# Attention with two mixtures of experts on one core: exponentials issued last in their step on ScalarE, and the placing product of v's block sums moved one step later into a bank of its own

## The chip, the cores and the metric

The kernel runs on one core of a Trainium2 chip. The metric is device microseconds (us) of one execution; lower is better.

## The reference

Three layers follow one another: a windowed attention, a soft mixture of experts over its output (3072 tokens of width 512, 32 slots), and a second mixture that sends each token to one expert. The change touches the attention and the first accumulation of the soft mixture, which runs along with it. What they compute:

```python
batch, n_heads, seq, head_dim = (4, 8, 768, 64)
block, window = (32, 16)
k_sum = k.reshape(B, H, nb, block, D).max(axis=3)      # nb = 24 blocks
v_sum = v.reshape(B, H, nb, block, D).mean(axis=3)
scores_l = scale * np.matmul(q, k.transpose(0, 1, 3, 2))   # masked to |i-j| < window
scores_s = scale * np.einsum('bhsd,bhnd->bhsn', q, k_sum) + np.log(block)
scores_all = np.concatenate([scores_l_m, scores_s], axis=-1)
a = np.exp(scores_all - np.max(scores_all, axis=-1, keepdims=True))
a = a / (np.sum(a, axis=-1, keepdims=True) + 1e-09)
attn = np.matmul(a, np.concatenate([v, v_sum], axis=2))
...
logits = x @ phi                        # soft mixture, x = attn as tokens
d = np.exp(logits - logits.max(0, keepdims=True))      # over all tokens
slot_input = (d / (d.sum(0, keepdims=True) + 1e-9)).T @ x
```

## The kernel before, in words

The 32 pairs of batch and head are taken two heads at a time: 16 pairs `n`, each cut into two halves of 384 rows. A half is a step `u` (0 to 31, pair `n = u // 2`), so even steps begin a pair. Ten more steps drain the pipeline and finish the soft mixture's slot inputs; after them come the expert weights' products and the second mixture, which the diff doesn't touch.

The order of instructions on each engine is the order in which the program issues them (a manual schedule). Each engine works through its own queue in that order, and an instruction that waits for data holds up all that stand behind it on the same engine. In the code, the loop over `u` calls in turn:

- `s_pe(u)`, line 302: 12 scores products on PE (24 matmul instructions, since one in this type takes two) into two banks, one for each head; they read q, and the windows of k together with the block maxima that `t_sum` has put into k's tile.
- `s_max(u, j)`, line 317: on DVE, scaling, mask and row minimum of the negated scores, three for each head, into the SBUF buffer `sms[u % 2]`.
- `s_exp(u, j)`: the row minimum is subtracted on POOL (line 330), then ScalarE takes the exponential (line 333), for each head.
- `v_pe(u - 2)`, line 354, and `v_norm(u - 2)`, lines 369 to 371: the product po of the transposed weights with v, and DVE's division by the sums.
- In odd steps, `vs(n)` and `vs2(n)` for the next pair but the current: `vs_pe` (line 249) sums v's blocks in 24 instructions into a bank `pv`; `vs_out` (line 257) copies that out on ScalarE; `vs_dist` (line 260) is a product with a 0/1 matrix that places each sum in the rows where it is needed, and writes to columns 256 to 385 of the same bank; a second `vs_out` copies that out, and `vs_in` (line 268) copies it into v's tile on POOL.
- `x_pe`, `x_ev`, `x_log`, lines 387, 397 and 405: transposes of the finished rows, ScalarE's copy, and the logits of the soft mixture.
- Once in eight steps the soft mixture's pieces: `moe_a` (steps 13, 21, 29, 37: column maxima, exponential, copy of the logits, correction of the running sum), `moe_b` (transposes of that, one step later), `moe_c` (product with the tokens, two steps after that), `moe_d`.
- `p_pe(u - 1)`, lines 341 and 342: transposes of the previous step's exponentials, and ScalarE's copies of them (`pts`).
- `t_sum(n + 1)` in odd steps, lines 277 to 286: on DVE the block maxima of the next pair's keys, in two levels; line 285 writes the part that the next step's first scores read, line 286 the rest.

PSUM banks: three in rotation (`ps_tr`, tag `tr`) for pv, the transposes and moe_b's and moe_c's products; three for the scores; one for po; one for the logits. A new tile waits until the one three before it has been read.

Loads are issued by SyncE (SP) in the same loop: keys, queries and v three pairs ahead, and one 1 MB tile of expert weights in most even steps from step 4 on; a load waits for its buffer's last reader.

Of the kernel before, what the change touches and what calls it, by code (L numbers as in the profile page):

```python
# [11 lines left out]
F32 = mybir.dt.float32  # L12
# [10 lines left out]
P = 128  # L23
B, H, S, D = 4, 8, 768, 64
# [28 lines left out]
C_DIST = C_BLK + 72  # L53
# [81 lines left out]
def tile_kernel(ctx, tc, qT, kTd, vwd, phi, w1, w2, emb, tau, u1, u2, consts, consts2, out):  # L135
    nc = tc.nc

    cp = ctx.enter_context(tc.tile_pool(name="cp", bufs=1))
    con = cp.tile([P, C_END], F32, name="con")
# [5 lines left out]
    nm_run = cp.tile([96, B], F32, name="nm_run")  # L145
# [58 lines left out]
    with ExitStack() as es:  # L204
        p3 = es.enter_context(tc.tile_pool(name="p3", bufs=3))
        p2 = es.enter_context(tc.tile_pool(name="p2", bufs=2))
        ps_tr = es.enter_context(tc.tile_pool(name="ps_tr", bufs=3, space=PSUM))
# [4 lines left out]
        st_ = {}  # L212
        NPAIR = B * 4
# [5 lines left out]
        sms = [fix[3][:, i * 6 * KW : (i + 1) * 6 * KW].rearrange("p (j c x) -> p j c x", j=2, c=3) for i in range(2)]  # L219
# [34 lines left out]

        def vs_out(n, i):
            sm = st_["vo", n]
            nc.scalar.copy(sm[:, 130 * i : 130 * i + 130], st_["pv", n][:, 256 * i : 256 * i + 130])  # L257

        def vs_dist(n):
            nc.tensor.matmul(  # L260
                st_["pv", n][:, 256:386], con[:, C_DIST : C_DIST + P], st_["vo", n][:, 0:130], start=True, stop=True
            )

        def vs_in(n):
            vo = st_.pop(("vo", n))
            for row0, par in ((32, 0), (96, 1)):
                eng = nc.vector if n == 0 and par else nc.gpsimd
                eng.tensor_copy(  # L268
                    st_["vw", n][row0 : row0 + NB, par].rearrange("p (s x) -> p s x", s=6),
                    vo[row0 : row0 + NB, 130:260].unsqueeze(1).to_broadcast([NB, 6, 130]),  # L270
                )
# [53 lines left out]
                    accum_out=st_["nb", u][:, j, c : c + 1],  # L325
                )

        def s_exp(u, j):
            sm = sms[u % 2][:, j]
            nc.gpsimd.tensor_tensor(  # L330
                out=sm, in0=sm, in1=st_["nb", u][:, j].unsqueeze(2).to_broadcast([P, 3, KW]), op=ALU.subtract
            )
            nc.scalar.activation(sm, sm, AF.Exp, scale=-1.0)  # L333

        def p_pe(u):
            pts = p2.tile([KW, 2, 3, P], F32, tag="pts", name=f"pts{u}")
            for j in range(2):
                pt = ps_tr.tile([P, 512], F32, tag="tr", name=f"pt{u}_{j}")[:KW, 0 : 3 * P]
                pt = pt.rearrange("p (c x) -> p c x", c=3)
                for c in range(3):  # L340
                    nc.tensor.transpose(pt[:, c, :], sms[u % 2][:, j, c, :], ident)  # L341
                nc.scalar.copy(pts[:, j], pt)  # L342
            st_["pts", u] = pts
# [69 lines left out]
        def moe_a(b):  # L413

            lp = st_.pop(("lp", b))
            LT = p2.tile([96, 2, 256], F32, tag="LT", name=f"LT{b}", bufs=1)
            nm, prev = nm_run[:, b : b + 1], nm_run[:, b - 1 : b]
            nc.vector.tensor_reduce(nm, lp, axis=AX.X, op=ALU.max, negate=True)
            if b:
                nc.vector.tensor_tensor(out=nm, in0=nm, in1=prev, op=ALU.min)  # L420
            nc.scalar.activation(LT[:, 1, :], lp, AF.Exp, bias=nm, scale=1.0, accum_out=sm_run[:, b : b + 1])
            nc.vector.tensor_copy(LT[:, 0, :], lp)
            if b:
                al = sp.tile([96, 1], F32, tag="al", name=f"al{b}")
                nc.scalar.activation(al, prev, AF.Exp, bias=nm, scale=-1.0)
                nc.vector.scalar_tensor_tensor(
                    out=sm_run[:, b : b + 1],
                    in0=sm_run[:, b - 1 : b],
                    scalar=al,
                    in1=sm_run[:, b : b + 1],  # L430
                    op0=ALU.mult,
                    op1=ALU.add,
                )
                st_["al", b] = al
                if b == B - 1:
                    dal = p3.tile([96, 96], F32, name="dal", bufs=1)
                    nc.vector.tensor_scalar_mul(dal, ident[:96, :96], al)
                    st_["dal"] = dal
            st_["LT", b] = LT

        def moe_b(b):
            LT = st_.pop(("LT", b))
# [8 lines left out]
        def moe_b_ev(b):  # L451
            L = sp.tile([P, 2, 2, 96], F32, tag="L", name=f"L{b}")
            pn = st_.pop(("pn", b))
            if b < B - 1:
                nc.vector.tensor_copy(L, pn)
            else:
                nc.vector.tensor_copy(L[:, 1], pn[:, 1])
                nc.scalar.copy(L[:, 0], pn[:, 0])
            st_["L", b] = L
# [120 lines left out]
        def keep_warm(n):  # L580

            pw = ps_o.tile([P, 3, 2, 65], F32, tag="po", name="warm1").rearrange("p a b x -> p (a b x)")
            for _ in range(n):
                nc.tensor.matmul(pw[:, 0:256], ident, con[:, C_MASK : C_MASK + 256], start=True, stop=True)  # L584

        def at(u, first, every, count):

            i, r = divmod(u - first, every)
            return i if r == 0 and 0 <= i < count else None
# [7 lines left out]
        last = B - 1  # L597

        def vs(n):
            vs_pe(n)  # L600
            vs_out(n, 0)

        def vs2(n):
            vs_dist(n)
            vs_out(n, 1)
            vs_in(n)

        for u in range(NU + 11):
            inr = lambda w: 0 <= w < NU
            m, odd = divmod(u, 2)  # L610
            if inr(u):
                s_pe(u)
                for j in range(2):
                    s_max(u, j)
                    s_exp(u, j)
            if inr(u - 2):
                if (u - 2) % 8 == 0:
                    st_["X", (u - 2) // 8] = xp.tile([P, 6, DM], F32, tag="X", name=f"X{(u - 2) // 8}")
                v_pe(u - 2)
                v_norm(u - 2)  # L620
            if u == 1:
                p_pe(0)
                vs(0)
                vs2(0)
                vs(1)
                vs2(1)
            vn = m + 1 if odd and 0 < m < NPAIR - 1 else None
            if vn is not None:
                vs(vn)
            if (n := at(u, 3, 2, NPAIR)) is not None:  # L630
                x_pe(n, 0)
                x_ev(n, 0)
            if (n := at(u, 4, 2, NPAIR)) is not None:
                x_pe(n, 1)
                x_ev(n, 1)
            if (n := at(u, 6, 2, NPAIR)) is not None:
                x_log(n)
            if (b := at(u, 13, 8, B)) is not None:
                moe_a(b)
            if (b := at(u, 14, 8, B - 1)) is not None:  # L640
                moe_b(b)
                moe_b_ev(b)
            if (b := at(u, 16, 8, B - 1)) is not None:
                moe_c(b)
                moe_c_ev(b)
            for i in range(3):
                if (b := at(u, 16 + i, 8, B)) is not None:
                    moe_d(b, i)
            if vn is not None:
                vs2(vn)  # L650
            if inr(u - 1) and u > 1:
                p_pe(u - 1)
            if odd and m + 1 < NPAIR:
                t_sum(m + 1)
            if u == U_END:
                keep_warm(2)
                si_max()
                si_max_ev()
                keep_warm(1)
                moe_b(last)  # L660
                moe_c(last, 0)
                keep_warm(1)
                moe_b_ev(last)
                si_bc()
                si_bc_ev()
                moe_c(last, 1)
                si_den()
                si_den_ev()
                moe_c(last, 2)
                moe_c_ev(last)  # L670
                keep_warm(1)
                siT_done()
                keep_warm(1)
            if u == 0:
                load_qk(2)
                load_v(2)
            if odd and m < NPAIR - 3:
                load_qk(m + 3)
                load_v(m + 3)
            if u == 3:  # L680
                nc.sync.dma_start(out=con[:, C_SEL:], in_=consts[:, C_SEL:])
                nc.sync.dma_start(out=phis, in_=phi.rearrange("(c p) s -> p c s", p=P))
            for _ in range(W_STEPS.count(u)):
                load_w()
# [128 lines left out]
    for r in range(2):  # L813
        for fc in range(8):
# [4 lines left out]
            for c in range(2 if late else 1):  # L819
                cs = slice(c * 256, c * 256 + 256) if late else slice(0, DM)  # L820
                for g in range(4):
# [4 lines left out]
                        start=(r, fc) in ((0, 0), (1, G_STEP + 1)),  # L826
                        stop=(r, fc) in ((1, G_STEP), (1, 7)),
# [19 lines left out]
            if r == 0 and fc % 2:  # L847
                b = fc // 2
# [4 lines left out]
            if 8 * r + fc in C_STEPS:  # L853
                b, j = divmod(C_STEPS.index(8 * r + fc), 2)
# [526 lines left out]
```

## Time and profile before

| what | value |
|---|---|
| runs of the kernel, median (lowest to highest of 3) | 293.59 us (292.58 to 293.78) |
| profiled execution, its own time | 292.89 us |
| span of the profiled execution | 291.1 us |
| mean granted TensorE clock | 0.958 of full speed |
| busy share of the span: PE, DVE, ACT, POOL | 84%, 53%, 44%, 31% |
| scores of step 2 start, scores of step 31 start | 16.81 us, 156.23 us |
| first product of the expert weights starts | 179.86 us |

Engines are PE (TensorE matmul), PEld (its weight loads, which overlap), DVE (VectorE), ACT (ScalarE), POOL (GpSimd) and SP. An instruction's row gives its start, its duration, engine, line, operation, what it writes and reads, and in brackets the time that its engine stood idle before it with the instruction that ended the wait. Matmuls are pipelined, so the duration of a group of them reaches into the next group; the distance from start to start tells what a group costs. Steps are cut at the first scores product (line 302): step 15 is 76.29 to 81.42.

### The profile page before, as it was taken

The numbers are of one execution on the slowest core, as the hardware profiler recorded it, in microseconds if no ns is written. First come the engines' busy times: TensorE is split into PE (matmuls) and PEld (weight loads), VectorE is DVE, ScalarE is ACT, GpSimd is POOL, SyncE is SP. The second block draws the span as 40 slices with busy tenths as digits, with TensorE's granted clock in tenths as the row PEclk, the third lists the DMA queues.
The fourth block names the chain that finished last, engine by engine and source line by source line (L and its number), as shares of the span: only waits on it lengthen the run. The fifth ranks groups of instructions, "written<-read, shape, count | busy, mean of one in ns | idle before, by whom it ended". The sixth has DMA issues, their size and how long they took to land.

```text
span 291.1 us, 7899 instructions
## 1 busy us (share of the span) xinstructions
PE 245.6 (84%) x3070; PEld 158.4 (54%) x3070; DVE 153.7 (53%) x699; ACT 127.7 (44%) x289; POOL 91.5 (31%) x131
## 2 busy tenths in 40 slices
PE   5688889896798886889868889999989999769980
PEld 1467666665566764656656454333256673536760
DVE  2366676666657666766666243115121467565850
ACT  1425655564454663355544331103322647923540
POOL 0455546554445544537444010000010272010000
PEclk9979999999999999999989799999999979986997
DMA  7997989999488996863485799999939200001993
GB/s 221 404 350 256 369 274 324 334 352 313 163 301 265 312 306 257 281 226 111 146 257 196 274 359 371 351 386 386 331 108 375 102 0 1 1 27 44 338 381 113
DMA packets 33658, 72.53 MB, mean 249 GB/s; under 512 B 2712, under 2 KB 4504, under 8 KB 33616
## 3 DMA queue, kind: packets, MB, share of 16 engines
q1 hardware_dynamic: 33552, 71.77, 70.1%
q8 instruction: 26, 0.43, 0.6%
q0 software_dynamic: 64, 0.20, 0.2%
q14 instruction: 16, 0.13, 0.1%
HBM read 65.67 MB, written 6.29 MB: 247 GB/s over the span
## 4 chain that ended last, share of the span: by engine, by line
PE 37%; DVE 5%; ACT 4%; DMA 3%; issue 2%; POOL 2%; SPq 1%; DVEq 0%; ACTq 0%; POOLq 0%
PE ph L746 5%; PE pO L822 4%; PE pht L1039 3%; DMA w2e<-in_moe_w_dram 3%; PE py L1282 2%; PE py L1284 2%; PE py L1283 2%; PE po L354 2%; DVE hlo L1052 2%; POOL fix L330 2%; PE s L302 1%; PE pa L476 1%; PE warm L584 1%; PE pc L194 1%; PE tx L387 1%
## 5 line engine op out<-in xcount | busy, mean ns | idle before, releaser
L333 ACT ACTIVATE fix<-fix 128x360 f32<-128x360 f32 x64 | 32.3, 504 | 74.9 <-POOL fix L330 74.9
L330 POOL TENSOR_TENSOR fix<-fix,nb 128x360 f32<-128x360 f32 x64 | 49.2, 789 | 48.0 <-DVE nb L317 48.0
L317 DVE CUSTOM_DVE_ANT_0 fix<-s,con 128x120 f32<-128x120 f32 x192 | 41.7, 279 | 40.5 <-PE s L302 39.3
L354 PE MATMUL po<-vw,pts 120*64 120x65 f32 x768 | 33.9, 236 | 7.3 <-ACT pts L342 6.7
L354 PEld LDWEIGHTS po<-vw,pts 120*64 120x64 f32 x768 | 27.8, 145 | 15.1 <-ACT pts L342 10.3
L268 POOL COPY vw<-vw 24x780 f32<-24x780 f32 x31 | 26.3, 848 | 28.1 <-issue 26.7
L342 ACT COPY pts<-pt 120x384 f32<-120x384 f32 x64 | 27.8, 483 | 6.2 <-PE pt L341 5.0
L341 PE MATMUL pt<-con,fix 128*120 128x128 f32 x192 | 27.9, 279 | 2.2 <-ACT xT L397 1.5
L341 PEld LDWEIGHTS pt<-con,fix 128*120 128x120 f32 x192 | 21.2, 138 | 9.4 <-issue 5.8
L302 PE MATMUL s<-fix,fix 64*64 64x120 f32 x480 | 18.4, 277 | 4.6 <-DVE fix L285 4.2
L387 PE MATMUL tx<-con,X 128*128 128x128 f32 x96 | 18.0, 298 | 0.7 <-DVE X L371 0.7
L371 DVE TENSOR_TENSOR X<-po,den 128x384 f32<-128x384 f32 x32 | 17.8, 558 | 1.1
L302 PEld LDWEIGHTS s<-fix,fix 64*64 64x64 f32 x480 | 13.4, 136 | 8.5 <-DVE fix L285 4.8
L1052 DVE CUSTOM_DVE_ANT_0 hlo<-pht,scr 128x1024 fp32r<-128x1024 f32 x11 | 13.3, 1212 | 8.6 <-PE pht L1039 8.5
L397 ACT COPY xT<-tx 128x384 f32<-128x384 f32 x32 | 15.1, 472 | 4.3 <-PE tx L387 4.3
L1039 PE MATMUL pht<-cT,gs 128*128 128x512 f32 x48 | 15.9, 454 | 0.7 <-ACT hhi L1063 0.5
L1063 ACT ACTIVATE hhi<-pht,scr 128x1024 fp32r<-128x1024 f32 x13 | 14.5, 1116 | 3.7 <-PE pht L1039 3.4
L317 DVE DVE_READ_ACCUMULATOR2_ANT nb<- 128x1 f32 x192 | 15.9, 83 | 0.0
L260 PE MATMUL pv<-vw,con 128*128 128x130 f32 x32 | 7.8, 326 | 9.3 <-ACT vw L257 9.3
L278 DVE TENSOR_REDUCE hm<-fix 128x48 f32<-128x768 f32 x16 | 15.1, 944 | 0.5 <-DMA fix<-in_kT_dram 0.5
L822 PE MATMUL pO<-w,hx 128*32 128x512 f32 (+1 forms) x152 | 15.4, 509 | 0.0
L746 PE MATMUL ph<-w,siT 128*32 128x512 f32 x128 | 14.8, 596 | 0.1
(232 smaller groups left out, 364.6 us busy)
## 6 DMA issues: line engine op xcount, KB each, us to landing
w<-in_moe_w_dram SPq DMA_DIRECT2D x30, 1024.0 KB, 8.8
vw<-in_vw_dram SPq DMA_DIRECT2D x32, 390.0 KB, 6.2
fix<-in_kT_dram SPq DMA_DIRECT2D x15, 484.0 KB, 4.6
out_dram<-Y SPq DMA_DIRECT2D x24, 256.0 KB, 2.9
fix<-in_qT_dram SPq DMA_DIRECT2D x15, 384.0 KB, 5.4
w1e<-in_moe_w_dram SPq DMA_DIRECT2D x4, 512.0 KB, 4.8
w2e<-in_moe_w_dram SPq DMA_DIRECT2D x4, 512.0 KB, 9.1
wx<-in_moe_w_dram SPq DMA_DIRECT2D x1, 1024.0 KB, 5.2
```

Source lines behind the costliest of these rows:

```text
L268: eng.tensor_copy(st_["vw", n][row0 : row0 + NB, par].rearrange("p (s x) -> p s x", s=6), vo[row0 : row0 + NB, 130:260].unsqueeze(1).to_br ...
L302: nc.tensor.matmul(sp[j][64 * i : 64 * i + 64, c, :], qns[n % 3][64 * j : 64 * j + 64, 64 * t : 64 * t + 64], kTs[n % 3][64 * j : 64 * j + ...
L317: nc.vector.tensor_tensor_reduce(out=sms[u % 2][:, j, c, :], in0=sp[:, c, :], in1=con[:, m0 : m0 + KW], scale=-0.125, scalar=3.0e38, op0=A ...
L330: nc.gpsimd.tensor_tensor(out=sm, in0=sm, in1=st_["nb", u][:, j].unsqueeze(2).to_broadcast([P, 3, KW]), op=ALU.subtract)
L333: nc.scalar.activation(sm, sm, AF.Exp, scale=-1.0)
L341: nc.tensor.transpose(pt[:, c, :], sms[u % 2][:, j, c, :], ident)
L342: nc.scalar.copy(pts[:, j], pt)
L354: nc.tensor.matmul(po[64 * i : 64 * i + 64, c, j, :], pts[:, j, c, 64 * i : 64 * i + 64], vw[:KW, i, x0 : x0 + 65], start=True, stop=True,)
L387: nc.tensor.transpose(pt[:, c * P : c * P + P], st_["X", b][:, c0 + c, hp * P : hp * P + P], ident)
L746: nc.tensor.matmul(ph[32 * g : 32 * g + 32, :], siT[:, kc, :], w[:, g, :], start=kc == 0, stop=kc == 3)
L822: nc.tensor.matmul(po[c][32 * g : 32 * g + 32, 0 : cs.stop - cs.start], hTs[r][:, fc, 32 * g : 32 * g + 32], w[:, g, cs], start=(r, fc) in ...
L1039: nc.tensor.matmul(ph[:, c * 512 : c * 512 + 512], G[:, k * P : (k + 1) * P], cTt(1024 * j + 512 * c, 512), start=True, stop=True,)
```

## The change

Each step's subtraction on POOL stays where it was, as `s_sub`; the exponentials `s_exp` are issued at the end of the step, on ScalarE behind the copies of the transposed weights of the step before and behind moe_a's exponential. The placing product of v's sums, its copy and POOL's copies into v's tile (`vs2`) move from the odd step in which the sums are made to the even step behind it; the product writes to a bank of its own, taken from the three in rotation, so that `pv` is given back after its one copy. For the second pair, the sums are made in step 2 and placed in step 3, where both were in step 1. One of the two copies into the first pair's v tile goes from DVE to ScalarE. moe_a comes behind the transposes; in it DVE's copy of the logits stands ahead of the exponential, and the correction of the running sum becomes `moe_a2`, called a step later behind moe_b (at the last batch in the same step).

```diff
@@ -254,18 +254,17 @@
 
         def vs_out(n, i):
             sm = st_["vo", n]
-            nc.scalar.copy(sm[:, 130 * i : 130 * i + 130], st_["pv", n][:, 256 * i : 256 * i + 130])
+            nc.scalar.copy(sm[:, 130 * i : 130 * i + 130], st_.pop(("pv", n))[:, 0:130])
 
         def vs_dist(n):
-            nc.tensor.matmul(
-                st_["pv", n][:, 256:386], con[:, C_DIST : C_DIST + P], st_["vo", n][:, 0:130], start=True, stop=True
-            )
+            pd = ps_tr.tile([P, 512], F32, tag="tr", name=f"pd{n}")
+            nc.tensor.matmul(pd[:, 0:130], con[:, C_DIST : C_DIST + P], st_["vo", n][:, 0:130], start=True, stop=True)
+            st_["pv", n] = pd
 
         def vs_in(n):
             vo = st_.pop(("vo", n))
             for row0, par in ((32, 0), (96, 1)):
-                eng = nc.vector if n == 0 and par else nc.gpsimd
-                eng.tensor_copy(
+                (nc.scalar.copy if n == 0 and par else nc.gpsimd.tensor_copy)(
                     st_["vw", n][row0 : row0 + NB, par].rearrange("p (s x) -> p s x", s=6),
                     vo[row0 : row0 + NB, 130:260].unsqueeze(1).to_broadcast([NB, 6, 130]),
                 )
@@ -325,11 +324,14 @@
                     accum_out=st_["nb", u][:, j, c : c + 1],
                 )
 
-        def s_exp(u, j):
+        def s_sub(u, j):
             sm = sms[u % 2][:, j]
             nc.gpsimd.tensor_tensor(
                 out=sm, in0=sm, in1=st_["nb", u][:, j].unsqueeze(2).to_broadcast([P, 3, KW]), op=ALU.subtract
             )
+
+        def s_exp(u, j):
+            sm = sms[u % 2][:, j]
             nc.scalar.activation(sm, sm, AF.Exp, scale=-1.0)
 
         def p_pe(u):
@@ -418,8 +420,12 @@
             nc.vector.tensor_reduce(nm, lp, axis=AX.X, op=ALU.max, negate=True)
             if b:
                 nc.vector.tensor_tensor(out=nm, in0=nm, in1=prev, op=ALU.min)
+            nc.vector.tensor_copy(LT[:, 0, :], lp)
             nc.scalar.activation(LT[:, 1, :], lp, AF.Exp, bias=nm, scale=1.0, accum_out=sm_run[:, b : b + 1])
-            nc.vector.tensor_copy(LT[:, 0, :], lp)
+            st_["LT", b] = LT
+
+        def moe_a2(b):
+            nm, prev = nm_run[:, b : b + 1], nm_run[:, b - 1 : b]
             if b:
                 al = sp.tile([96, 1], F32, tag="al", name=f"al{b}")
                 nc.scalar.activation(al, prev, AF.Exp, bias=nm, scale=-1.0)
@@ -436,7 +442,6 @@
                     dal = p3.tile([96, 96], F32, name="dal", bufs=1)
                     nc.vector.tensor_scalar_mul(dal, ident[:96, :96], al)
                     st_["dal"] = dal
-            st_["LT", b] = LT
 
         def moe_b(b):
             LT = st_.pop(("LT", b))
@@ -612,7 +617,7 @@
                 s_pe(u)
                 for j in range(2):
                     s_max(u, j)
-                    s_exp(u, j)
+                    s_sub(u, j)
             if inr(u - 2):
                 if (u - 2) % 8 == 0:
                     st_["X", (u - 2) // 8] = xp.tile([P, 6, DM], F32, tag="X", name=f"X{(u - 2) // 8}")
@@ -622,9 +627,11 @@
                 p_pe(0)
                 vs(0)
                 vs2(0)
+            vn = m + 1 if odd and 0 < m < NPAIR - 1 else None
+            if (not odd and 1 < m < NPAIR) or u == 3:
+                vs2(m)
+            if u == 2:
                 vs(1)
-                vs2(1)
-            vn = m + 1 if odd and 0 < m < NPAIR - 1 else None
             if vn is not None:
                 vs(vn)
             if (n := at(u, 3, 2, NPAIR)) is not None:
@@ -635,24 +642,27 @@
                 x_ev(n, 1)
             if (n := at(u, 6, 2, NPAIR)) is not None:
                 x_log(n)
-            if (b := at(u, 13, 8, B)) is not None:
-                moe_a(b)
             if (b := at(u, 14, 8, B - 1)) is not None:
                 moe_b(b)
                 moe_b_ev(b)
+                moe_a2(b)
             if (b := at(u, 16, 8, B - 1)) is not None:
                 moe_c(b)
                 moe_c_ev(b)
             for i in range(3):
                 if (b := at(u, 16 + i, 8, B)) is not None:
                     moe_d(b, i)
-            if vn is not None:
-                vs2(vn)
             if inr(u - 1) and u > 1:
                 p_pe(u - 1)
+            if (b := at(u, 13, 8, B)) is not None:
+                moe_a(b)
+            if inr(u):
+                for j in range(2):
+                    s_exp(u, j)
             if odd and m + 1 < NPAIR:
                 t_sum(m + 1)
             if u == U_END:
+                moe_a2(last)
                 keep_warm(2)
                 si_max()
                 si_max_ev()
```

## Rows read from the trace of the kernel before

**Rows 1.** The page's first line: span of the profiled execution.
```profile
span 291.1 us, 7899 instructions
```

**Rows 2.** Waits, 0 to 160 us: engine, line, releaser: total us, times, longest.
```profile
PE pv L260 <- ACT vw L257: 9.3, 15, 1.3
```

**Rows 3.** Timeline of step 15: start us, duration us, instructions, [idle before <-releaser].
```profile
76.29 0.85 PE L302 MATMUL s<-fix,fix 64*64 64x120 f32 x24
...
77.06 0.92 PE L354 MATMUL po<-vw,pts 120*64 120x65 f32 x24
...
77.91 0.88 PE L249 MATMUL pv<-vw,con 120*32 120x130 f32 x24
...
79.41 0.16 DVE L277 TENSOR_REDUCE hm<-fix 128x1 f32<-128x16 f32 x1
...
79.64 0.50 ACT L333 ACTIVATE fix<-fix 128x360 f32<-128x360 f32 x1 [0.24 <-POOL fix L330]
80.05 0.25 ACT L257 COPY vw<-pv 128x130 f32<-128x130 f32 x1
...
80.35 0.49 PE L260 MATMUL pv<-vw,con 128*128 128x130 f32 x2 [1.08 <-ACT vw L257]
80.47 0.18 DVE L285 TENSOR_TENSOR fix<-hm 128x24 f32<-128x24 f32 x1
...
80.68 0.82 PE L341 MATMUL pt<-con,fix 128*120 128x128 f32 x6
81.42 0.85 PE L302 MATMUL s<-fix,fix 64*64 64x120 f32 x24
```

**Rows 4.** Windows by step: busy us (instructions) per engine, granted clock, DMA share, GB/s.
```profile
16.81:21.56 4.75, 4.30 (x54) 3.48 (x54) 2.92 (x16) 0.50 (x1) 3.02 (x4) 0.64 0.89 346
...
55.74:60.89 5.15, 4.35 (x85) 3.30 (x84) 3.56 (x19) 3.64 (x10) 1.81 (x4) 1.00 0.94 287
60.89:64.36 3.47, 3.47 (x65) 2.49 (x64) 2.13 (x15) 1.25 (x4) 3.04 (x4) 1.00 0.96 369
64.36:71.29 6.93, 4.41 (x85) 3.30 (x84) 4.56 (x21) 4.57 (x13) 3.20 (x4) 1.00 0.93 307
71.29:76.29 5.00, 4.23 (x68) 2.98 (x68) 2.85 (x17) 1.76 (x4) 1.53 (x2) 1.00 0.65 248
...
143.48:150.60 7.12, 4.41 (x84) 3.30 (x84) 4.90 (x23) 4.69 (x14) 3.21 (x4) 1.00 0.49 161
150.60:156.23 5.63, 5.63 (x68) 4.27 (x68) 2.94 (x17) 1.70 (x4) 1.53 (x2) 0.70 1.00 322
156.23:160.93 4.70, 2.83 (x59) 2.38 (x58) 2.13 (x15) 2.44 (x7) 1.54 (x2) 1.00 0.39 130
160.93:167.28 6.35, 6.06 (x51) 3.38 (x51) 1.92 (x5) 1.29 (x4) 0.00 (x0) 0.73 0.77 270
```

**Rows 5.** Timeline from the end of step 13 into step 14.
```profile
69.24 0.42 DVE L422 COPY LT<-lp 96x256 f32<-96x256 f32 x1 [1.09 <-ACT LT L421]
...
69.48 1.72 POOL L268 COPY vw<-vw 24x780 f32<-24x780 f32 x2 [1.80 <-issue]
...
70.63 0.60 DVE L285 TENSOR_TENSOR fix<-hm 128x24 f32<-128x24 f32 x1
...
71.29 1.05 PE L302 MATMUL s<-fix,fix 64*64 64x120 f32 x24 [1.72 <-DVE fix L285]
...
72.27 0.92 PE L354 MATMUL po<-vw,pts 120*64 120x65 f32 x24
```

**Rows 6.** Timeline of step 1.
```profile
11.95 0.88 PE L249 MATMUL pv<-vw,con 120*32 120x130 f32 x24
...
13.77 0.28 ACT L257 COPY vw<-pv 128x130 f32<-128x130 f32 x1
...
14.10 0.49 PE L260 MATMUL pv<-vw,con 128*128 128x130 f32 x2 [1.28 <-ACT vw L257]
...
14.93 0.56 DVE L268 COPY vw<-vw 24x780 f32<-24x780 f32 x1 [3.34 <-ACT vw L257]
```

## The prediction, made before the changed kernel was run

> **What bounds the kernel now.** I read the page first: a span of 291.1 us [rows 1] inside an execution of 292.89, against a median of 293.59 (292.58 to 293.78). The sum below is made against this execution and then carried over to the median, 0.70 higher. TensorE (PE) is busy for 84% of the span, so the question is where it stands still in the attention steps, the only ones that change.
>
> The list of waits gives the main place. The placing product of v's sums (line 260) kept PE waiting 15 times, 9.3 us in all, for ScalarE's copy of the sums [rows 2]. The timeline of step 15 shows why [rows 3]: the sums' product (pv, line 249) was done by 78.8, but its copy (line 257) starts at 80.05, right behind the second exponential of the step (79.64), which had waited for POOL's subtraction. PE idles 1.08 us, since all its matmuls stand in one queue.
>
> Cutting the windows at each step's first scores matmul (line 302) shows two kinds of step [rows 4]. Even ones without extra work, like 60.89 to 64.36, take 3.47 us with PE busy for all 3.47: nothing can be won there. Odd ones, like 55.74 to 60.89, take 5.15 with PE busy for 4.35 (5.13 to 5.15 from step 7 on, 5.14 below). The three odd steps in which moe_a runs take 6.93 to 7.12 (first and last of them are the windows from 64.36 and 143.48).
>
> Then comes the row that limits the gain. In step 15 VectorE (DVE) starts the next pair's key maxima (t_sum, line 277) at 79.41, and line 285, which the next step's first scores need, ends at 80.65 [rows 3]. That is 4.36 after the step's own first scores; in step 14 the scores start 0.06 after line 285 has ended [rows 5]. So however fast PE and ScalarE become, an odd step that is followed by a new pair can't be shorter than about 4.42 us.
>
> **The change part by part.**
>
> *Ordinary odd steps* (ten: 5, 7, 9, 11, 15, 17, 19, 23, 25, 27). The placing product goes, with its wait of 1.08 and its issue time of 0.33 (80.35 to 80.68). PE alone would need 5.14 - 1.08 - 0.33 = 3.73. The maxima allow 4.42. I take 4.42: -0.72 each, -7.2 in all. The ends are 3.73 (a further -6.9 over ten steps, excluded as long as line 285 stands where it is in the scores' operands) and 5.14 (no gain).
>
> *Even steps* (4, 6, 8, 10, 12, 16, 18, 20, 24, 26, 28) receive the product: +0.33, on a queue that is already full. They also start behind the maxima, so line 286 follows: in step 14, which starts so, po begins 0.98 after the scores (71.29 to 72.27), in step 15 0.77 after [rows 3, 5]. That is +0.21. Together +0.54 in eleven steps, +5.9. The most part of the ordinary steps' gain is thus given back: 5.14 + 3.47 = 8.61 per pair becomes 4.42 + 4.01 = 8.43.
>
> *Steps 13, 21, 29 (moe_a).* DVE's copy of the logits waited 1.09 for ScalarE's exponential of the same tile [rows 5]; now it comes first, and the correction of the running sum moves to the next step. What also goes is a collision: line 285 took 0.60 in place of 0.18 because POOL's copies of v's sums (line 268, 69.48 to 71.20) were running; they now belong to even steps. 1.09 + 0.42 = 1.5 each, -4.5 in all (ends -1.3 and -1.7 each).
>
> *Steps 14, 22, 30.* PE is busy for 4.23 of 5.00 [rows 4]. The remaining 0.77 is a transpose that needs a bank which ScalarE frees only behind its exponentials; that order is what changes. With +0.33 for the product: -0.44 each. Step 30 runs at a granted clock of 0.70 and takes 5.63; after a shorter wait I expect it at full clock, 4.56: -1.07. Together -1.95 (if the clock still falls, -0.9 from the first two).
>
> *Step 31.* 4.70 with PE busy for 2.83, so 1.87 of waiting for the copies that stand behind the exponentials. Copies behind only their transposes still cost some 0.75 (half of the transposes' 0.82 and the second copy, which I price by the exponential's 0.50): -1.1. The stretch from 160.93 ran at 0.73; whether the shorter wait keeps the clock up is open: between 0 and -1.7 (all of 0.27 x 6.35), taken -0.7.
>
> *Start.* In step 1 the copy of v's sums starts at 13.77, though pv ended at 12.83; the placing product follows at 14.10; DVE's own copy (14.93) had waited 3.34 and holds back t_sum, and the second pair's sums are made before step 2's scores at 16.81 [rows 4, 6]. Afterwards: the copy at 12.9, the placing product from 13.2, step 2's scores at about 13.65, since t_sum no longer stands behind that copy. Its po then waits for the copies of v's sums at about 15.1; po 0.86, pv 0.8 (now here) and transposes 0.81 put step 3 at 17.6 against 21.56: -3.9 at full clock. This stretch was granted 0.64 before [rows 4], and PE will idle here again, so I take -3.0, with ends -2 and -3.9. The copy that moves to ScalarE isn't in the trace: 780 elements by the exponential's 0.50 for 360 are at most 1.08, by DVE's 0.56 at least that; POOL's copy beside it took 1.15, which hides either. In step 3 POOL's copies still fall on t_sum, so I give that step no gain.
>
> *Tail.* At the last moe_a ScalarE's exponential comes behind DVE's copy (0.42), with everything up to the slot inputs behind it: +0.4.
>
> *At nothing:* the exponentials' later place (rival three prices it) and the extra bank, whose earlier users have been copied out about a step before. No DMA is added or moved, but the key loads wait for the scores and the weight loads for po, so they come earlier with the steps. An ordinary pair moves 287 GB/s and 369 GB/s in its two steps, 320 over both; 2% less time makes 327, under the 369 of the second step, so they stay hidden [rows 4].
>
> Sum: -3.0 - 7.2 + 5.9 - 4.5 - 1.95 - 1.1 - 0.7 + 0.4 = -12.15. From 292.89 that gives 280.7, in terms of the median **281.4 us**.
>
> **The rivals.**
>
> *One: the maxima don't end sooner (17%).* For it: line 285's stretch to 0.60 beside POOL's copy. If POOL's copies slide so far that they meet t_sum in every odd step, ten times 0.42 returns: 285.6; if odd steps keep 5.14 altogether, 281.4 + 7.2 = 288.6. Against it: POOL's two subtractions are over before t_sum begins, and two copies of 0.86 behind them in an even step run about 1 us into the next odd one, whose t_sum starts 3.1 in. The Trainium skill, "SBUF — State Buffer", section "SBUF: two separate sides", says that VectorE and GpSimd share a pair of ports as an exclusive lock, held for a whole instruction. The trace agrees: line 285 ended 0.03 after POOL's copies.
>
> *Two: the clock falls at the odd steps' wait (8%), the other side.* PE will stand still for about 0.7 in one piece at the end of each odd step. A fall cost step 30 1.4 us of PE time (5.63 against 4.23 for the same work in step 14). Nine falls in thirteen odd steps use up the 12.15; thirteen give 281.4 + 18.2 = 299.6. For it: step 30 after a longer wait. Against it: 1.08 in step 15 and 1.72 before step 14 left the clock at 1.00 [rows 3 to 5]. The Trainium skill, "TensorE: Matmul & The Clock Gate", Part 1, calls the low clock the default, which activity releases. That speaks for this rival in kind; these two rows speak against it in size.
>
> *Three: the exponentials come too late for the next step's transposes (8%).* The transposes start 0.74 before a step's end (80.68 to 81.42), in an even one some 3.3 in; with 0.82 for them, 0.50 for the last copy and 1.0 for two exponentials, ScalarE is done at about 5.6. The next step's transposes come at 4.01 + 2.98 = 7.0, so 1.4 to spare; from an odd step 2.4. Only if ScalarE ran later than that by 0.4 in each of 30 steps would all be gone: 293.
>
> *Four: more than forecast (5%)*: the maxima don't bind and odd steps go to PE's 3.73: 281.4 - 6.9 = 274.5.
>
> **How the numbers follow.** The forecast has 62%; with all its terms at their good ends it gives 278.9, at their bad ones 284.8. The range leaves out the best rival below and, above 288, the two worst with some of rival one: 278 to 288. A measurement of this kernel tells about 0.5%, 1.5 us, from no change. Faster: 62 + 17 + 5 = 84%; same: most of rival three, 7%; slower: rival two and the rest, 9%.
>
> **What would show it.** Right: line 260 no longer waits for line 257; odd steps last about 4.4 and end with PE waiting 0.6 to 0.7 for line 285; plain even steps last 4.0 with PE full; steps 13, 21 and 29 last about 5.5; step 3 starts near 18. Wrong: odd steps near 3.7 or above 4.8; line 285 above 0.18 outside step 3; the transposes (line 341) waiting for line 333's exponentials; a granted clock under 1.00 in steps 5 to 29. The prediction fails most easily by the clock at the start and the end, some 2 us, and by t_sum.

## The result and the profile after

The changed kernel takes 275.36 us (median of 4 runs, 274.06 to 275.72) against 293.21 for the kernel before, timed along with it: a ratio of 0.9384, 95% interval 0.9346 to 0.9422. That is faster, as forecast, but by 17.85 us where 12.15 were forecast, and 2.6 us below the range.

The page of the changed kernel: its span, TensorE's busy time, and the granted clock in 40 slices.

```profile
span 273.4 us, 7963 instructions
...
PE 237.8 (87%) x3070; PEld 156.3 (57%) x3070; DVE 152.0 (56%) x698; ACT 127.1 (46%) x290; POOL 90.9 (33%) x131
...
PEclk9999999999999999999999999999999979977997
```

The span is 17.7 shorter than that of [rows 1], and the clock stands at 9 (90% or more) in every slice to the end of attention.

Waits of the changed kernel in the first 150 us (engine, line, releaser: total us, times, longest). Line numbers have moved: the scores are line 301, t_sum's operations 276 to 285, the placing product 261, po 356, the transposes 343, the exponentials 335.

```profile
PE s L301 <- DVE fix L284: 12.7, 14, 1.6
...
PE pt L343 <- ACT fix L335: 0.7, 2, 0.5
...
PE pd L261 <- ACT vw L257: 0.4, 1, 0.4
```

The wait of [rows 2], 9.3 us in 15 places, has shrunk to 0.4 in one. In its place PE waits for the block maxima: 14 times, 12.7 us. The transposes waited for exponentials twice, 0.7 in all, both in the first steps.

Windows by step, columns as in [rows 4]: steps 2, 13, 14, 15, 18, 30, 31 and 32.

```profile
13.53:17.38 3.85, 3.31 (x79) 2.64 (x79) 2.22 (x15) 2.50 (x6) 2.37 (x3) 1.00 1.04 400
...
59.22:64.30 5.08, 3.80 (x83) 2.99 (x82) 3.97 (x21) 3.71 (x11) 2.89 (x4) 1.00 0.98 342
64.30:68.57 4.27, 4.27 (x69) 3.27 (x69) 2.83 (x17) 1.54 (x5) 2.18 (x3) 1.00 0.96 344
68.57:72.99 4.42, 3.64 (x83) 2.97 (x82) 3.32 (x20) 3.16 (x9) 2.56 (x4) 1.00 0.77 260
83.06:87.00 3.94, 3.94 (x65) 2.94 (x65) 2.81 (x18) 1.80 (x6) 1.84 (x3) 1.00 0.98 356
137.25:141.53 4.28, 4.28 (x70) 3.28 (x70) 2.85 (x18) 1.33 (x5) 2.19 (x3) 1.00 0.98 330
141.53:144.88 3.35, 2.83 (x59) 2.39 (x58) 2.32 (x17) 2.63 (x8) 2.53 (x4) 1.00 0.94 306
144.88:149.69 4.81, 4.52 (x51) 2.40 (x51) 1.92 (x5) 1.90 (x6) 0.03 (x1) 1.00 0.96 318
```

Step 15 (68.57) takes 4.42 and the plain even step 18 (83.06) 3.94, full. Steps 13 and 14 take 5.08 and 4.27 where they took 6.93 and 5.00; step 30 takes 4.28 for 5.63, and the clock is 1.00 in all of them.

The timeline of step 15 and the start of step 16, to be held against [rows 3].

```profile
68.57 0.85 PE L301 MATMUL s<-fix,fix 64*64 64x120 f32 x24
...
69.35 0.92 PE L356 MATMUL po<-vw,pts 120*64 120x65 f32 x24
...
70.20 0.88 PE L249 MATMUL pv<-vw,con 120*32 120x130 f32 x24
...
71.14 0.27 ACT L257 COPY vw<-pv 128x130 f32<-128x130 f32 x1 [1.08 <-PE pv L249]
...
71.69 0.16 DVE L276 TENSOR_REDUCE hm<-fix 128x1 f32<-128x16 f32 x1
...
72.72 0.91 ACT L335 ACTIVATE fix<-fix 128x360 f32<-128x360 f32 x2
72.75 0.18 DVE L284 TENSOR_TENSOR fix<-hm 128x24 f32<-128x24 f32 x1
...
72.99 1.05 PE L301 MATMUL s<-fix,fix 64*64 64x120 f32 x24 [0.78 <-DVE fix L284]
...
74.82 0.49 PE L261 MATMUL pd<-vw,con 128*128 128x130 f32 x2
```

The copy of the sums (71.14) now starts 0.94 after pv's first matmul and stands behind nothing; the exponentials come after the copies, at 72.72; line 284 starts 4.18 after the step's scores, as before, and the next scores 0.06 after its end, 0.78 after PE was free. In step 16 the placing product follows po.

Cut at the same places, the difference is:

| part | forecast us | measured us |
|---|---|---|
| start, up to step 3's scores (21.56, now 17.38) | -3.0 | -4.2 |
| step 3 | 0 | -0.6 |
| ten ordinary odd steps | -7.2 | -7.3 |
| eleven even steps | +5.9 | +5.8 |
| steps 13, 21, 29 | -4.5 | -5.55 |
| steps 14, 22, 30 | -1.95 | -2.8 |
| step 31 | -1.1 | -1.35 |
| step 32 (6.35, now 4.81) | -0.7 | -1.5 |
| steps 33 to the first product of the expert weights | +0.4 | +0.2 |
| all after that | 0 | -0.3 |
| sum (of the unrounded parts) | -12.15 | -17.7 |

### The profile page after: what moved, and what is told of

The parts are those of the page before. It is cut to its first block, busy times and chain, and to the rows that moved or that the text cites. A ratio compares the mean times of both kernels' runs of the same rounds, so it can differ in the third digit from the quotient of the medians.

```text
span 273.4 us, 7963 instructions
## 1 busy us (share of the span) xinstructions
PE 237.8 (87%) x3070; PEld 156.3 (57%) x3070; DVE 152.0 (56%) x698; ACT 127.1 (46%) x290; POOL 90.9 (33%) x131
## 4 chain that ended last, share of the span: by engine, by line
PE 62%; DVE 23%; DMA 4%; issue 3%; ACT 3%; POOL 1%; SPq 1%; DVEq 0%; ACTq 0%
PE s L301 10%; DVE fix L316 7%; PE po L356 5%; PE ph L756 5%; PE pt L343 5%; PE pO L832 5%; DVE hm L277 4%; PE pht L1049 4%; PE lp L407 3%; DVE X L373 3%; DMA w2e<-in_moe_w_dram 3%; PE pa L481 3%; PE py L1292 2%; PE pd L261 2%; PE py L1294 2%
## 5 line engine op out<-in xcount | busy, mean ns | idle before, releaser
L335 ACT ACTIVATE fix<-fix 128x360 f32<-128x360 f32 x64 | 29.2, 510 | 8.3 <-POOL fix L329 8.3
L356 PE MATMUL po<-vw,pts 120*64 120x65 f32 x768 | 29.9, 226 | 1.4 <-POOL vw L267 0.5
L356 PEld LDWEIGHTS po<-vw,pts 120*64 120x64 f32 x768 | 25.3, 137 | 6.9 <-ACT pts L344 3.1
L343 PE MATMUL pt<-con,fix 128*120 128x128 f32 x192 | 27.1, 276 | 0.7 <-ACT fix L335 0.7
L301 PE MATMUL s<-fix,fix 64*64 64x120 f32 x480 | 19.0, 272 | 8.3 <-DVE fix L284 7.9
L301 PEld LDWEIGHTS s<-fix,fix 64*64 64x64 f32 x480 | 14.0, 132 | 12.7 <-DVE fix L284 10.0
L389 PE MATMUL tx<-con,X 128*128 128x128 f32 x96 | 16.7, 283 | 0.7 <-DVE X L373 0.7
L257 ACT COPY vw<-pd 128x130 f32<-128x130 f32 x16 | 4.3, 268 | 25.6 <-PE pd L261 25.6
L301 PE MATMUL s<-fix 64*64 64x120 f32 x288 | 11.4, 272 | 5.5 <-DVE fix L284 4.8
```

Of the source, the lines that this page charges most:

```text
L301: nc.tensor.matmul(sp[j][64 * i : 64 * i + 64, c, :], qns[n % 3][64 * j : 64 * j + 64, 64 * t : 64 * t + 64], kTs[n % 3][64 * j : 64 * j + ...
L356: nc.tensor.matmul(po[64 * i : 64 * i + 64, c, j, :], pts[:, j, c, 64 * i : 64 * i + 64], vw[:KW, i, x0 : x0 + 65], start=True, stop=True,)
```

## The experiments

Twelve runs followed. Theory A: PE stood still because of the order in ScalarE's queue; after the change odd steps are bound by DVE's block maxima and even ones by PE. The rivals were B (POOL's copies and t_sum meet), C (the clock) and D (the rotation of three banks).

### The three parts one at a time

*Exponentials only*: the kernel before, with

```diff
-                    s_exp(u, j)          # subtraction and exponential
+                    s_sub(u, j)          # subtraction
...
                 p_pe(u - 1)
+            if inr(u):
+                for j in range(2):
+                    s_exp(u, j)          # exponential alone
```

> The kernel before with one part of the change: the exponentials behind ScalarE's copies of their step; v's sums are still placed in the same odd step, moe_a is as before. Theory A (what cost time was the order in ScalarE's queue): the copy of v's sums no longer stands behind the exponentials, so the placing product waits 0.1 us or less; odd steps come down to the 4.4 that line 285 of before sets, even ones stay near 3.6, step 31 loses about 1.3, the stretch after it about 1.5 if the clock stays full: 280 us, most of the gain. Rival B (POOL's copies of v's sums now run just when t_sum's last two operations need DVE's and POOL's common port, since the second copy on ScalarE ends about 3.6 into the odd step): line 285 or 286 stretches by 0.4 to 0.9 in every odd step, odd steps last 4.8 to 5.3, and the whole is 285 to 290 us.

Measured: 282.35 us (277.82 to 285.69) against 293.41. Its runs spread with the granted clock, from 0.983 in the shortest to 0.946 in the longest, so no interval is given. An ordinary pair takes 4.73 + 3.67 = 8.40. The time lies between the two expectations. The timeline of step 11 shows A, and a milder form of B:

```profile
55.85 0.49 PE L260 MATMUL pv<-vw,con 128*128 128x130 f32 x2
...
56.77 1.79 POOL L268 COPY vw<-vw 24x780 f32<-24x780 f32 x2
57.14 0.50 DVE L285 TENSOR_TENSOR fix<-hm 128x24 f32<-128x24 f32 x1
...
57.70 1.05 PE L302 MATMUL s<-fix 64*64 64x120 f32 x24 [0.64 <-DVE fix L285]
```

The placing product follows tx without a wait, but line 285 lasts 0.50 in place of 0.18: it ends at 57.64, as the first of POOL's two copies does (56.77 and half of the 1.79 that both took). The odd step is 0.31 longer than 4.42 for that.

*Placing product only*: `vs2` moved to the even step with a tile `pd` of its own, and the start, all else as before.

> The kernel before with one part: the placing product of v's sums a step later in its own bank (start included); the exponentials stay in front on ScalarE, moe_a as before. Theory A: odd steps still wait for the copies behind the exponentials (po by about 0.4), even steps become 4.0; ordinary pairs gain nothing, only the start gives about 3 to 4 us and moe_a's collision on POOL 0.4 three times: 287 to 290 us. Rival (the placing product itself was what held PE): 282 us or less.

Measured: 296.45 us (295.56 to 296.82), ratio 1.0096 (1.0062 to 1.013). Both theories missed: it is slower. A pair takes 4.61 + 4.54 = 9.15. One wait (in the first 160 us) holds nearly all of it:

```profile
PE pt L340 <- ACT vw L257: 17.3, 23, 1.3
```

The transposes now wait for ScalarE's copy of v's sums. The three banks hold pv (or pd), tx and the transposes' two halves in turn, so the second half gets the bank of pv or pd, which is free only when that copy, behind the exponentials, is done.

*moe_a only*: DVE's copy ahead of the exponential, the running sum a step later, moe_a behind the transposes; all else as before.

> The kernel before with one part: moe_a behind the transposes, its DVE copy of the logits ahead of the exponential, the correction of the running sum a step later. Theory A: DVE no longer waits about 1 us in steps 13, 21 and 29, but POOL's copies still meet t_sum there and PE still waits for the copies of v's sums: 1.0 to 1.5 us in each of the three steps, 0.4 to 0.7 more if step 30 keeps the full clock: 288 to 290 us. If the wait was covered by another one as long: 293.

Measured: 288.69 us (285.89 to 289.31), ratio 0.981 (0.9753 to 0.9867), as expected. Step 13 takes 5.90 for 6.93.

*Banks*: the placing product only, and four banks in rotation with two for the scores.

```diff
-        ps_tr = es.enter_context(tc.tile_pool(name="ps_tr", bufs=3, space=PSUM))
-        ps_s = es.enter_context(tc.tile_pool(name="ps_s", bufs=3, space=PSUM))
+        ps_tr = es.enter_context(tc.tile_pool(name="ps_tr", bufs=4, space=PSUM))
+        ps_s = es.enter_context(tc.tile_pool(name="ps_s", bufs=2, space=PSUM))
```

> The later placing product alone (as in the run that was 1% slower than before), with four banks in rotation for the transposes, sums and placing products and two for the scores. Theory D (alone it lost time because it puts one tile more into the rotation of three banks, while ScalarE still copies late: the second half of the transposes waits for the copy of v's sums, 0.83 us in odd and 0.57 in even steps): those waits go, even steps come from 4.54 to about 4.0, odd ones to between 4.4 and 4.6, 288 to 290 us. Rival (the product's place on PE itself costs it): no gain over 296.

Measured: 291.43 us (288.27 to 294.26), ratio 0.9887 (0.984 to 0.9935). Two of its waits in the first 160 us:

```profile
PE s L301 <- PE pt L340: 6.0, 11, 0.9
...
PE pt L340 <- ACT vw L257: 0.2, 1, 0.2
```

17.3 us of waiting for line 257 have become 0.2, ordinary even steps take 3.90 for 4.54 and odd ones 4.54 for 4.61. That confirms D. The gain is 1.4 us short of the expected band, and the second row is new: scores that wait behind the transposes, 6.0 us.

### The change without one part

*Without the later placing product* (it is back in the odd step and in pv's bank; the start is as before):

> The changed kernel without the later placing product (it stands in the odd step and in pv's bank, as before, and step 1 is as before): the exponentials behind the copies, and moe_a's new order. Theory A (with the exponentials late, the placing product's move is worth the start, where step 3 of the exponentials' run began 2.7 us later than the changed kernel's, and little else, since an ordinary pair took 8.40 us there against 8.36): 278 to 279 us. Rival (the parts need each other): 281 or more.

Measured: 277.88 us (275.72 to 280.01), ratio 0.9426 (0.9358 to 0.9495), just under A's band. This interval overlaps the changed kernel's, so in the whole time the worth of the placing product's part is likely but not shown. Where it counts is the start. Step 2 of this kernel, and of the one with the exponentials alone, which has the same start:

```profile
16.12:20.56 4.44, 3.99 (x55) 3.14 (x55) 3.04 (x16) 1.04 (x3) 3.03 (x4) 0.71 1.02 397
...
16.78:20.07 3.29, 2.83 (x54) 2.21 (x55) 2.34 (x15) 0.79 (x3) 2.20 (x3) 1.00 1.04 404
```

Step 3 begins at 20.56 here, 3.2 later than in the changed kernel, but at a clock of 0.71 in step 2. At 1.00, as in the changed kernel, it begins at 20.07, 2.7 later; 1.0 of that was lost before the two kernels differ (pv of step 1 starts at 12.81, in the changed kernel at 11.85), so about 1.7 is the part's own. Ordinary pairs take 8.40 against 8.36.

*Without moe_a's new order*:

> The changed kernel with moe_a as before (ahead of the transposes, exponential first, running sum at once). Theory A: DVE waits again for ScalarE's exponential in steps 13, 21 and 29, now behind fewer instructions than before, 0.9 to 1.2 us in each: 278 to 279 us. Rival (that wait is hidden once the exponentials are late): 275.5.

Measured: 279.45 us (277.56 to 282.95), ratio 0.9513 (0.9436 to 0.959), so moe_a's part is worth some 1.5% in the whole. Steps 13 and 14 of the profiled execution, the longest of the four:

```profile
59.63:65.43 5.80, 3.64 (x83) 2.97 (x82) 4.06 (x21) 4.34 (x12) 2.89 (x4) 1.00 1.00 363
65.43:71.25 5.82, 5.82 (x69) 4.56 (x70) 2.93 (x17) 0.91 (x3) 3.19 (x4) 0.71 0.74 276
```

Step 13 is 0.72 longer than in the changed kernel (steps 21 and 29: 0.85 each), less than A's 0.9 to 1.2. In this execution the clock also fell behind those longer waits: steps 14, 22 and 30 ran at 0.71, 0.55 and 0.71 and took 5.82, 6.94 and 5.81, where the changed kernel took 4.27 to 4.28 at 1.00.

*The changed kernel again*, on one chip with the four-bank kernel above and the last two kernels below:

> The changed kernel once more, beside the others of this job, for comparing on one chip: 274 to 276 us.

Measured: 275.3 us (273.87 to 280.24), ratio 0.936 (0.928 to 0.9441), as expected. One of its four executions took 280.24 at a mean clock of 0.958; the other three had 0.975 to 0.986. The long one isn't traced, so where its clock was low isn't known.

### The clock

The kernel before, with work for PE in two of its long waits:

```diff
+            if u == 30:                     # ahead of step 30's scores
+                for _ in range(3):
+                    nc.tensor.matmul(sp[0][:, 0:256], ident, con[:, C_MASK : C_MASK + 256], start=True, stop=True)
...
+                if u == 32:                 # the same into a scores bank, ahead of v_pe(30)
```

> The kernel before with three extra products on PE, whose results nobody reads, ahead of step 30's scores and three ahead of step 32's v product, so that PE works while it would wait; all else as before. Theory C (the low clock in these two stretches comes from PE's long waits, and costs some 0.8 to 1.4 us in each): granted clock 1.00 in both, step 30 about 5.0 and the step from 160.93 about 5.0 long: 291 us. Rival (the clock falls there for another reason, or the extra products cost as much as they give): 293 or more.

Measured: 291.39 us (289.79 to 292.43), ratio 0.9927 (0.99 to 0.9953). Windows of steps 14, 22, 30 and 32 of this kernel:

```profile
72.13:77.77 5.64, 5.45 (x68) 4.09 (x68) 2.94 (x17) 1.81 (x4) 1.54 (x2) 0.74 0.62 238
112.42:118.06 5.64, 5.64 (x68) 4.27 (x68) 2.95 (x17) 1.67 (x4) 1.53 (x2) 0.70 0.57 215
152.72:157.72 5.00, 4.22 (x67) 2.99 (x67) 2.86 (x17) 1.76 (x4) 1.53 (x2) 1.00 1.02 334
162.43:167.42 4.99, 4.70 (x51) 2.45 (x52) 1.92 (x5) 1.29 (x4) 0.00 (x0) 1.00 1.00 353
```

Steps 30 and 32 are at 1.00 and last 5.00 and 4.99, where they had 0.70 and 0.73 and lasted 5.63 and 6.35 [rows 4]. In this execution the clock fell in steps 14 and 22 instead, behind waits of 1.72 and 1.90; in the kernel before both ran at 1.00 behind the same two waits. So whether such a wait lets the clock fall differs from run to run, and one trace doesn't show that the extra products kept it up. The ten executions speak for C: 0.7% shorter, clear of no change, with mean clocks of 0.958 to 0.971 where the kernel before beside them had 0.942 to 0.959. The low clock of step 14 costs 0.64 (5.64 for 5.00).

### What bounds the changed kernel

*POOL's copies alone in the even step*; product and copy go back to the odd one:

```diff
+            if vn is not None:              # odd: product and ScalarE's copy
+                vs_dist(vn); vs_out(vn, 1)
...
-                vs2(m)                      # even
+                vs_in(m)                    # even: POOL's copies
```

> The changed kernel with the placing product and its copy back in the odd step (in a bank of its own), only POOL's copies into v's tile in the even step. Theory A (odd steps have 0.7 us of PE time to spare behind t_sum, even ones none): odd steps stay at 4.42, even ones lose the product's 0.33 and come to about 3.65, line 284 stays at 0.18: 13 to 14 times 0.3, 271 us. Rival (the three banks in rotation, now four tiles in odd steps, make the transposes wait for ScalarE): 275 or more.

Measured: 273.22 us (269.99 to 274.6), ratio 0.9267 (0.9177 to 0.9357). Steps 15 and 18:

```profile
67.57:71.98 4.41, 4.09 (x84) 3.18 (x83) 3.31 (x20) 3.04 (x9) 2.83 (x4) 1.00 0.91 297
81.79:85.46 3.67, 3.67 (x63) 2.67 (x63) 2.55 (x17) 1.70 (x5) 1.57 (x3) 1.00 0.90 308
```

As A says, step by step: the odd step stays at 4.41 with 0.32 of PE time to spare, the even one falls to 3.67. Step 31 starts at 138.37 for 141.53, but of these 3.2 us only 2.0 were left at the end of the profiled execution (271.4 for 273.4), lost after attention, where the edit changes nothing (the last 43.4 us were granted 0.80 here and 0.88 there). The two kernels' intervals overlap, so in the whole time the gain is likely but not shown.

*Maxima in the even step*: the changed kernel, with

```diff
-            if odd and m + 1 < NPAIR:
+            if u == 1 or (not odd and 0 < m < NPAIR - 1):
                 t_sum(m + 1)
```

> The changed kernel with one more edit: the next pair's block maxima (t_sum) are made at the end of the even step and not of the odd one, from the second pair's on. Theory A (odd steps are bound by DVE's chain up to t_sum's third operation, even ones by PE): the odd steps' wait of 0.78 goes and even steps lose the 0.2 of their late second part, so odd steps last about 3.75 and even ones 3.75; with 13 such pairs about 10 us less than the changed kernel, 265 us, or 268 if POOL's copies of v's sums, which then run beside t_sum, hold DVE up so that the odd steps' maxima of the scores come late. Rival (something else in the odd steps, the exponentials or the copies, stands right behind t_sum): 273 us or more.

Measured: 261.26 us (260.15 to 263.81), ratio 0.8918 (0.8853 to 0.8983), the fastest of all. Steps 7 and 8:

```profile
33.41:36.97 3.56, 3.56 (x82) 2.96 (x81) 2.96 (x18) 2.31 (x7) 3.05 (x4) 1.00 1.01 359
36.97:40.71 3.74, 3.74 (x66) 2.76 (x65) 2.66 (x17) 2.40 (x7) 1.82 (x3) 1.00 1.01 382
```

PE is busy for the whole of both; a pair takes 7.30 for 8.36. The time is 3.7 us below A's 265: A counted thirteen pairs alike, and the odd steps with moe_a fell by more (step 13 from 5.08 to 3.57).

*Early maxima without the later placing product, and with the product back in the odd step:*

> The kernel with the block maxima made in the even step, without the later placing product (it stands in the odd step and in pv's bank, step 1 as before): exponentials behind the copies, moe_a's new order, early maxima. Theory A (once PE is full in both steps, the product costs its 0.33 in either): pairs stay near 7.3 to 7.5, only the start loses some 3 us: 264 to 266 us. Rival (the product waits again for the copy in the fuller odd step, or POOL's copies hold v's rows up): pairs of 7.9 or more, 271 us or more.

> The early maxima together with the placing product back in the odd step and POOL's copies in the even one. Theory A: PE full in both steps, so the 0.33 is only moved: pairs near 7.3, 260 to 262 us, within 0.5% of the early maxima alone. Rival (the product's place still matters): 3 us or more to either side.

Measured: 262.38 us (261.13 to 266.06), ratio 0.8933 (0.8858 to 0.9008), under its band; and 264.26 (262.18 to 264.58), 0.8989 (0.8921 to 0.9058), above its band. Both have pairs of 4.02 + 3.47 = 7.49, not 7.30: with PE full in both steps, the product costs 0.46 in the odd step and saves 0.27 in the even one, in pv's bank and in one of its own alike. The 0.33 that the product itself takes is the same in both places. The other 0.19 is in its neighbours, counted from start to start: with the product in the odd step, tx takes 0.45 there and the transposes of the exponentials (pt) 0.81, without it 0.39 and 0.74; in the even step tx takes 0.48 behind po and 0.42 behind the product. Why that is so was not settled. Of the three kernels, none can be told from the others by its interval. Step 2 of the last one:

```profile
15.54:20.32 4.78, 4.78 (x80) 3.95 (x79) 3.00 (x17) 2.49 (x6) 2.36 (x3) 0.63 1.03 400
```

Up to here PE is given the same instructions as in the changed kernel, which had 1.00 in this step; the clock had fallen in step 1 already (0.57 from 12.0 to 13.5 us).

## Why the prediction was wrong

The mechanism was right, and so was the bound: odd steps end at the maxima, 4.42, and the even steps give much of that back. What the forecast named as signs came: no wait of line 260, PE waiting 0.78 for line 285 of before, step 3 at 17.4. That the sums over the ten odd and the eleven even steps came out to 0.1 us is partly luck: a plain even step rose by 0.47, not by 0.54, and step 4's 1.12 made up for it; step 23 fell by 0.45 only (4.69), and step 5's 1.06 made up for that.

**The step that failed is the sizes of the other terms, 5.55 us in all and all to the same side:** the clock, priced at a hedge at the start and in step 32 (2.0 of the 5.55); the chain of steps 13, 21 and 29, of which a part was left out (1.05); busy time taken for length in steps 14, 22 and 30 (0.85); and step 3, put at nothing (0.6).

*Start (-3.0 taken, -4.2 measured).* The working gave -3.9 at full clock. I held back 0.9 because the stretch had been at 0.64 before. It ran at 1.00, and that was in part luck: the last kernel above, the same up to there on PE, had 0.63 and began step 3 at 20.32, 2.9 later, 0.7 of it lost before the clock fell (scores of step 1 at 10.05 for 9.31). Of the six traced executions with this start and late exponentials five ran at 1.00. At equal clock the placing product's part is worth some 1.7 of the 4.2.

*Step 32 (-0.7, of 0 to -1.7; -1.5 measured).* The same hedge on the clock, and here the change itself settles it. In the nine traced executions with late exponentials PE waits 0.52 ahead of this step, and it lasts 4.80 to 4.82 at 1.00. In the four with the exponentials in front and no extra products the wait is 1.87 to 1.94, and it lasts 6.35 to 6.59 at 0.73 to 0.74 in three and 5.00 at 1.00 in one.

*Steps 13, 21, 29 (-1.5 each, -1.85 measured).* I counted DVE's wait of 1.09 and the collision on line 285. Left out was po's wait for the copies, visible in the rows: it delays DVE's division and with it t_sum. Of the kernel before, po and DVE's maximum in step 13, then that maximum and the copy of the logits in the changed kernel:

```profile
65.61 1.18 PE L354 MATMUL po<-vw,pts 120*64 120x65 f32 x24 [0.41 <-ACT pts L342]
...
67.74 0.41 DVE L418 TENSOR_REDUCE nm_run<-lp 96x1 f32<-96x256 f32 x1
```
```profile
62.34 0.41 DVE L420 TENSOR_REDUCE nm_run<-lp 96x1 f32<-96x256 f32 x1
62.67 0.41 DVE L423 COPY LT<-lp 96x256 f32<-96x256 f32 x1
```

po came 1.25 after the step's scores (step 15: 0.77), the maximum 3.38, now 3.12: 0.26. From the maximum to the copy it was 1.50 [rows 5], now 0.33: 1.17. With the collision's 0.42 that is the 1.85. In steps 21 and 29 the correction of the running sum, which leaves the step, is 0.13 of it; step 13, the first batch, has none. The 4.42 of the ordinary steps was read from step 15, where po didn't wait.

*Steps 14, 22, 30 (-0.44 twice and -1.07; -0.73, -0.72 and -1.35).* I added 0.33 to PE's 4.23 busy us and got 4.56; measured 4.27. The busy time of a step whose transposes are split by a wait counts the modelled ends of both halves, 0.49 and 0.54 in step 14 of before; in one piece all six take 0.75 from start to start.

*Step 3 (0, -0.6).* POOL's copies did fall on t_sum there, as forecast, but on its second part: line 285 of the changed kernel lasted 0.95, while line 284, which the next scores wait for, started at 21.66, where the first of the two copies ends (20.83 and half of 1.72), and took its 0.18. So this step, too, ended 0.06 behind line 284.

*Step 31 (-1.1, -1.35).* The working's sum is off: half of 0.82 and 0.50 are 0.91, not 0.75. Measured, the copies no longer set the step: PE waits 0.52 for DVE's division.

*Range.* Its good end, 278.9, let only the start, steps 13, 21 and 29 and step 32 come out better; all other terms stood as exact on that side.

**The rivals.** *One* is real but hardly here: of the changed kernel's t_sum operations only line 285 in step 3 was stretched by POOL's copies beyond 0.3. With the exponentials alone moved it happens in ordinary odd steps, for 0.32 in most: line 285 of that kernel took 0.50 in place of 0.18, until the POOL copy that was running had ended (57.64). The Trainium skill, "SBUF — State Buffer", section "SBUF: two separate sides", has the two engines share ports as a lock held for an instruction; the trace agrees by these 0.50 us. *Two* didn't come in the two traced executions: no fall from step 2 to step 32, behind waits of up to 1.64. It isn't excluded for others: the one execution at 280.24 had a mean clock of 0.958. The price of a fall held where PE fills the step: step 14 of the kernel with the exponentials alone took 5.39 at 0.69, its steps 22 and 30 took 4.00 and 4.01 at 1.00. *Three*: transposes waited 0.7 in all. *Four*: odd steps do go below 4.42 once the maxima leave them, which this change doesn't do.

**What the forecast did not see**: I put the extra bank down at nothing. That holds only because the exponentials moved too. Alone, the placing product's move made the kernel 1% slower by the rotation of banks; the exponentials alone already removed most of the wait of [rows 2] (0.8 in two places were left of 9.3).

## What to carry to other kernels

When a wait goes, look for the instruction that is ready last behind it, on another engine: here line 285 set the odd steps to the hundredth, and moving that chain into the slack of the step before gave a further 14 us. Before moving work to another stage of a rotation, count its tiles against the buffers and ask which copy frees each one. For a step with extra waits, count from start to start and not from busy time, and give the terms with rows an error too.

## What the runs showed of the hardware

A fall of the clock to its lower level differed between executions of nearly the same program: step 14, behind a wait of 1.72, ran at 1.00 in the kernel before and at 0.74 in the one with extra products in steps 30 and 32 only. Counted over the traces, steps 14, 22 and 30 ran at 1.00 in all twelve cases behind waits of 0.75 to 1.64 (the changed kernel twice, POOL's copies alone in the even step, and the one without the later placing product) and in four of fourteen behind waits of 1.72 to 2.49 (the kernel before, with extra products, the exponentials alone, the placing product alone, and without moe_a's new order). That is a count, not a rule. Runs of one kernel (the exponentials alone) lay between 277.8 and 285.7 us, with mean clocks of 0.983 and 0.946.

VectorE got in between two GpSimd copies that followed each other directly: line 285 in step 11 of the exponentials' run was held up for the rest of the first copy (0.50 in place of 0.18), not for both (1.79).
